# Attention with normalized q and k: shifted fp16 patterns as 64-bit adds on GpSimd, the rest of its work on VectorE

## The chip, the cores and the metric

The kernel runs on one core of a Trainium2 chip. The metric is the device time in microseconds, the median of the runs. A profiled execution is taken beside them; its rows give the engines' instructions with start and duration. The engines are TensorE (PE in the profile, PEld its weight loads), VectorE (DVE), ScalarE (ACT), GpSimd (POOL) and SyncE (SP), which here only issues DMAs.

## The reference

32 heads, 2048 positions, head dimension 20, bfloat16. Rows of q and k are normalized to length one, the scores are scaled by a factor per head, and plain attention follows:

```python
qn = q / (jnp.sqrt((q * q).sum(axis=-1, keepdims=True)) + eps)
kn = k / (jnp.sqrt((k * k).sum(axis=-1, keepdims=True)) + eps)
logits = jnp.einsum('bhqd,bhkd->bhqk', qn, kn) * t[None, :, None, None]
attn = _softmax(logits, axis=-1)
return jnp.einsum('bhqk,bhkd->bhqd', attn, v)
```

Scores are bounded by t, a little above 1, so the kernel takes no maximum. v has a column of ones beside it (`vaug`), so that the product with the exponentials yields the row sums too, and the division comes at the end.

## The kernel before

**Two ways to an exponential.** Each head's 2048 x 2048 scores are cut into 16 tiles by key block; a tile is 128 keys by 2048 queries, in four groups of 512 queries. TensorE makes the scores (L762). For most tiles ("A") ScalarE takes the exp out of PSUM into `p_ring` (L853), in waves of two and three groups in turn (128x1024 and 128x1536). For the others ("D") VectorE makes a cheap exponential: it reads the scores out of PSUM, two instructions of 128x1024 a tile, and writes an int16 which is, read as fp16, a piecewise linear power of two (`xt`, L909). To smooth it, three more patterns are made by adding 256, 512 and 768 to that integer (`ss`, L916, one instruction of 128x2048 each), that is the same curve shifted in phase; they are multiplied with copies of v scaled by 2^(-phase/1024) (`vph`, L577), and TensorE adds all four products up in `psO` (L782). `DVE_TILES` says how many of the 16 tiles of each head are D tiles: 158 in all, the other 354 are ScalarE's.

**GpSimd's part.** A shift may also go to GpSimd (`f.alt`, L920): two int16 lanes are added at once as one int32, as a tensor-tensor add whose second operand is a constant of `add_w` with step zero; so a tile of 2048 int16 is 1024 words, and it may be cut into pieces of at least 128 words. GpSimd also scales the copies of v (`vs`, L577, three a head), folds the squares of q and k twice before VectorE sums them (`fold`, L615), normalizes q and k from head 3 on (`norm`, L657) and divides by the row sums (`fin`, L806, heads 1 to 30).

**The order of work** is written out ahead of time by a list scheduler in the kernel's own file (`Program`): each task has an engine, a duration, dependences and a due time in units of heads (`pri`, small is early), and each engine then runs its tasks in the scheduler's order, with semaphore waits for the dependences. So every engine's queue is strictly in order: an instruction that waits holds all behind it. `pool_fill` places GpSimd's work: a piece is given to GpSimd when VectorE begins an instruction that reads PSUM (`t1`, L909), a transpose (`tr`, L795) or a sum (`su`, L622), and it is cut to the length which should end with that instruction (`piece`, 0.02 us and `PRATE` us a word, after 0.3 us of lead, or none where the wait can be taken earlier); VectorE's other instructions start, in the plan, only after such a piece. A shift goes to GpSimd only if VectorE has other work waiting (`KEEP`).

**Preparation of a head** runs some three heads ahead (`LEAD` 3.2): loads, squares (L607), sums, an inverse square root in integer and float steps (L626 to L644), normalization, then on SP's queue a transposing DMA into `qkT` (L675) and DMAs that lay out `qz` and the rotated copies `kR`. From head 5 on two heads are prepared together. v is loaded into one of six buffers; the scaled copies follow.

The lines that the change and the prediction's steps touch: L577 (`vs`), L615 (`fold`), L622 (sum), L657 and L664 (`norm` on GpSimd and on VectorE), L806 (`fin`), L916 and L920 (shift on VectorE and on GpSimd), L909 (PSUM read), L853 (exp).

Of the kernel before, what the change touches and what calls it, by code (L numbers as in the profile page):

```python
# [11 lines left out]
F32 = mybir.dt.float32  # L12
I32 = mybir.dt.int32
I16 = mybir.dt.int16
ACT = mybir.ActivationFunctionType
AXIS_X = mybir.AxisListType.X

# [2 lines left out]

KEXP = 0.2403756
PHASES = (256, 512, 768)
LOG2E = math.log2(math.e)
RS_MAGIC = 1594963007.0
RS_K1 = -2.253391575687845
# [20 lines left out]
class Program:  # L46
# [12 lines left out]
    PE_REST = 4.2  # L59
    PV_SLACK = 0.6  # L60
    OVER = 0.03
    PRATE = 0.00164
    KEEP = 0.3
    RESTP = 0.3
    SPARE = 0.0
# [10 lines left out]
    def add(self, eng, name, fn, dur, deps=(), pri=0.0, lat=0.0, dma=None):  # L76
        t = Task(eng, name, fn, dur, deps, pri, lat, dma)
        self.tasks.append(t)
        return t
# [310 lines left out]
def bass_standalone__qk_norm__prompt_kernel(  # L390
# [17 lines left out]
    NV = 6  # L408
# [14 lines left out]
    PE_MM = 0.23  # L423
    MORE = 12
    DLM = 2
    DVE_TILES = [4, 4, 4, 5, 4, 5, 5, 5, 5, 5, 5, 5, 5, 5, 6, 5, 5, 6, 5, 5, 3, 5, 5, 5, 6, 5, 4, 6, 5, 5, 6, 5]
    NDMAX = 6
    NPOOL, FPOOL = True, True
    FUSE, FOLD = True, 2
    NQ, NSQ, NSTEP = 2, 4, 0.0  # L430
    EXP0 = 0.051
    RSPOOL = False
    RTPOOL = False
    VPRI = 0.3
    LGATE = 0
    TTRATE = 0.00168
    TTDUR, TTWIN = 0.8, 0.55
# [2 lines left out]
    with ExitStack() as es:  # L440
        sbuf = lambda name, shape, dt: es.enter_context(nc.sbuf_tensor(name, shape, dt))
# [3 lines left out]
        t_f32 = sbuf("t_f32", [128, H], F32)  # L445
        act_scr = sbuf("act_scr", [128, 32], F32)
        ones = sbuf("ones", [128, 512], BF16)
        add_w = sbuf("add_w", [128, len(PHASES)], I32)
        ident = sbuf("ident", [128, 128], BF16)
        qk_sb = sbuf("qk_sb", [128, NB * 2 * R, D], BF16)  # L450
        vaug = [sbuf(f"vaug{i}", [128, R, 32], BF16) for i in range(NV)]
# [10 lines left out]
        xt = [sbuf("xt", [128, NX * 2048], I16)]  # L462
# [10 lines left out]
        add = prog.add  # L473
# [4 lines left out]
        def memset(eng, ap, val, dur, pri):  # L478
            return add(eng, "z", lambda e, tk: e.memset(ap, val), dur, pri=pri)
# [20 lines left out]
        while not waves or waves[-1][-1] < NA - 1:  # L500
            i = waves[-1][-1] + 1 if waves else 0
# [3 lines left out]
        for h in range(H):  # L505
            i = d0[h]
# [11 lines left out]
        add("ACT", "warm", lambda e, tk: e.activation(act_scr[:, :], act_scr[:, :], ACT.Exp), 1.5, [scr0], -95)  # L518
        ld_t = dma("SP", "ld_t", tb16[:, :], bass.AP(t.tensor, 0, [[0, 128], [1, H]]), [], -40, "t")
        z_one = memset("DVE", ones[:, :], 1.0, 0.2, -99)  # L520
        for i, x in enumerate(PHASES):
            memset("POOL", add_w[:, i:i + 1].bitcast(I16), x, 0.1, -98)
        z_id = add("POOL", "id", lambda e, tk: e.affine_select(
            ident[:, :], ones[:, 0:128], [[1, 128]], ALU.is_equal, 0.0, base=0, channel_multiplier=-1), 0.5, [z_one], -99)
        z_kx = memset("DVE", kx[:, :].rearrange("p (r w) -> p r w", w=32)[:, :, D:32], 0.0, 0.5, -97)
# [6 lines left out]
        z_v = []  # L532
# [6 lines left out]
        lds, ld_v, norm, trn, rot = {}, {}, {}, {}, {}  # L539
# [14 lines left out]
        def add_loads(h):  # L554
            b, bv = (h + 1) % NB, h % NV
            pri = h - LEAD - 0.5
            war = (norm[h - NB] if h >= NB else []) + ([lambda: [trn[max(h - 3, 0) if h < 5 + LGATE else h - 4]]] if h >= EARLY else [])
            x = qk_of(h)
            lds[h] = [dma("SP", f"ldk{h}", x[:, R:2 * R, :], k[0, h].rearrange("(p r) d -> p r d", p=128),
                          war, pri - 0.01 if h else -50, f"k{b}", lat=4.5 if h else 2.2, dur=0.5)]  # L560
            if h == 0:
                lds[h].append(dma("ACT", "ldq0", x[:, 0:R, :], q[0, 0].rearrange("(p r) d -> p r d", p=128),
                                  [], -99, "q0a"))
            else:

                for nh in range(4):
                    src = bass.AP(q.tensor, q[0, h].offset + nh * D,
                                  [[16 * D, 32], [4 * D, 4], [512 * D, 4], [1, D]])
                    dst = x[32 * nh:32 * nh + 32, 0:R, :].rearrange("p (c g) d -> p c g d", g=4)
                    lds[h].append(dma("SP", f"ldq{h}", dst, src, war, pri, f"q{b}", lat=4.5, dur=0.68))  # L570
            war = (pv_users[h - NV] if h >= NV else z_v[bv]) + ([lambda: [trn[h - 2]]] if h >= 2 else [])
            if h == 1:
                war = war + [lambda: [trn[0]]]
            ld_v[h] = dma("SP", f"ldv{h}", vaug[bv][:, :, 0:D], v[0, h].rearrange("(p r) d -> p r d", p=128),
                          war, pri + VPRI, f"v{bv}", lat=2.6, dur=1.4)
            nd = 4 if h < DLM else DVE_TILES[h]
            vsc[h] = [add("POOL", f"vs{h}", lambda e, tk, i=i: e.tensor_scalar(  # L577
                vph[bv][:, i, 0:nd, :], vaug[bv][:, R - nd:R, :], 2.0 ** (-PHASES[i] / 1024.0), 1.0, ALU.mult, ALU.mult),
                0.4, [ld_v[h]] + (pv_users[h - NV] if h >= NV else z_v[bv]), pri + 0.2) for i in range(len(PHASES))]
            for u in vsc[h] if h else []:  # L580
                u.win = 0.14

        def add_prep(hs):
            due = hs[0] - LEAD if hs[0] != 1 else FIRST
# [293 lines left out]
        def add_dgroup(jg):  # L878
            js = D_groups[jg]
            sx = se = 0  # L880
            ox, oe = place(0, NX, len(js)), place(1, NE, len(js))
            bx, be = 2048 * ox, 2048 * oe
            w = 2048 * len(js)
            old = lambda n, i: last_use.get((n, (ox if n == "x" else oe) + i), [])
            new = {}
            t1s = []
            for i, j in enumerate(js):
                h, rg = D_tiles[j]
                due = h + (j - d0[h] + 0.3) / DVE_TILES[h] - DLEAD
                n1 = W1 // 512  # L890
                for k in range(0, NG, n1):
                    gs = GORD[k:k + n1]
                    slot = nchunk[0] % (1024 // W1)
                    nchunk[0] += 1

                    def f_qk(eng, rows, h=h, rg=rg, gs=gs, slot=slot):
                        last = None
                        for m, g in enumerate(gs):
                            o = slot * W1 + 512 * m
                            last = qk_mm(eng, h, rg[g], g, psD[:, o:o + 512], rows)  # L900
                        return last
                    deps = [t1_prev.get(nchunk[0] - 1024 // W1)] + (q0 if j == 0 else [])
                    for g in gs:
                        deps += qk_deps([(h, rg[g], g)])
                    qk = add("PE", f"qkD{j}.{k}", lambda e, tk, f=f_qk: f(e, tk.rows), PE_MM, deps, due - 20000.0)
                    qk.modes = [("q2", 64, PE_MM, 256.0 * n1), ("qk", 128, PE_MM * n1, 512.0 * n1)]
                    qk_users[h].append(qk)
                    o = bx + 2048 * i + 512 * k
                    t1_prev[nchunk[0]] = add("DVE", f"t1.{j}.{k}", lambda e, tk, o=o, slot=slot: e.tensor_scalar(  # L909
                        xt[sx][:, o:o + W1], psD[:, slot * W1:slot * W1 + W1], X_MUL, X_ADD, ALU.mult, ALU.add),  # L910
                        0.067 + W1 / 960.0, [qk] + old("x", i), due - 5)
                    t1s.append(t1_prev[nchunk[0]])
            sh = []
            for i in range(len(PHASES)):
                dst, w = ss[i][0], 2048 * len(js)
                f = add("DVE", f"s{i}.{js[0]}", lambda e, tk, i=i, dst=dst: e.tensor_scalar(  # L916
                    dst[:, be:be + w], xt[0][:, bx:bx + w], float(PHASES[i]), None, ALU.add), 0.068 + w / 3840.0,
                    t1s + [u for m in range(len(js)) for u in old(f"s{i}", m)], due)
                if len(js) == 1 and jg >= 2:
                    f.alt = lambda c, n, i=i, dst=dst: lambda e, tk: e.tensor_tensor(  # L920
                        dst[:, be + 2 * c:be + 2 * (c + n)].bitcast(I32), xt[0][:, bx + 2 * c:bx + 2 * (c + n)].bitcast(I32),
                        bass.AP(add_w, i, [add_w[:, :].ap[0], [0, n]]), ALU.add)
                sh.append([(list(range(len(js))), f)])
            for m in range(len(js)):
                new["x", ox + m] = [u for us in sh for ms, u in us if m in ms]
            for i, j in enumerate(js):
                h, rg = D_tiles[j]
                for nm, tile, dep, ph in [("x", xt[sx], t1s[2 * i:2 * i + 2], None)] + [
                        (f"s{n}", ss[n][se], [u for ms, u in sh[n] if i in ms], n) for n in range(len(PHASES))]:
                    p = add("PE", f"pv{nm}{j}", lambda e, tk, h=h, rg=rg, o=2048 * i + (bx if ph is None else be), tile=tile, ph=ph: pv_mm(  # L930
                        e, h, lambda g: rg[g],
                        lambda g: tile[:, o + 512 * GORD[g]:o + 512 * GORD[g] + 512].bitcast(FP16), ph),
                        PE_MM, dep + pv_base(h) + (vsc[h] if ph is not None else []), due + 0.2)
                    pv_users[h].append(p)
                    new.setdefault((nm, (ox if nm == "x" else oe) + i), []).append(p)
            last_use.update(new)
# [76 lines left out]
```

## Time and profile before

| | us |
|---|---|
| median of 3 runs | 655.32 (655.14 to 655.39) |
| the profiled execution's span | 654.0 |
| first exp starts, last exp ends, in it | 8.42, 649.65 |
| GpSimd busy with shift pieces (L920, 314 pieces) | 311.4 |
| GpSimd busy with normalization (L657), folds (L615), v copies (L577), division (L806) | 47.7, 44.8, 40.0, 27.4 |
| VectorE busy with PSUM reads (L909), shifts (L916) | 384.8, 239.1 |

In the profile's groups a row gives line, engine, operation, the tiles written and read, the commonest shape and the count; then the time that the group was busy, the mean of one in ns, and the engine's idle time before them with what ended it. In the timeline a row gives start and duration in us. The TensorE clock row gives the granted clock in 40 slices, 9 for full speed.

### The profile page before, as it was taken

Reading aid. Unit: us, or ns where it says so; the run is one execution under the profiler, and the core shown is the slowest. Engines: PE = TensorE matmul, PEld = TensorE weight load, DVE = VectorE, ACT = ScalarE, POOL = GpSimd, SP = SyncE. Lnnn points to the kernel's source line nnn. Section 1 sums busy time; section 2 is a strip of 40 time slices with the busy share of each in tenths; the row PEclk is TensorE's granted clock in tenths of the full one; section 3 lists DMA queues with packets and bytes.
Section 4 is the critical chain, followed back from the end, with each engine's and each line's share of the span. In section 5 each row is a group of like instructions: output and inputs, shape, how many; then the busy total and the mean of one; then the engine's idle time right before and its main releaser. Section 6 shows DMA issues by size and latency. Waiting matters only on the chain.

```text
span 654.0 us, 14865 instructions
## 1 busy us (share of the span) xinstructions
PE 590.3 (90%) x5991; PEld 168.9 (26%) x6019; DVE 646.1 (99%) x911; ACT 647.4 (99%) x576; POOL 472.7 (72%) x550
## 2 busy tenths in 40 slices
PE   8888889899899898899999998989999989989997
PEld 2222222222222222222222222222222222222222
DVE  8999999999999999999999999999999999999998
ACT  9999999999999999999999999999999999999997
POOL 2577765777778776777877767768787876777773
PEclk9999999999999999999999989999999999999999
DMA  5554435342431535325242251354304334040200
GB/s 65 81 71 64 74 55 81 45 81 22 83 57 27 92 37 74 48 56 75 32 87 31 54 76 27 73 62 74 55 18 81 42 66 64 18 85 12 49 13 11
DMA packets 196724, 36.25 MB, mean 55 GB/s; under 512 B 172592, under 2 KB 196656, under 8 KB 196656
## 3 DMA queue, kind: packets, MB, share of 16 engines
q1 hardware_dynamic: 196512, 35.22, 35.0%
q8 instruction: 47, 0.77, 0.5%
q14 instruction: 21, 0.17, 0.1%
q10 hardware_dynamic: 144, 0.08, 0.0%
HBM read 7.87 MB, written 2.62 MB: 16 GB/s over the span
## 4 chain that ended last, share of the span: by engine, by line
ACT 97%; PE 2%; DVE 0%; issue 0%; ACTq 0%
ACT p_ring L853 96%; PE psO L782 1%; PE psA L762 1%; ACT qz L529 0%; ACT L518 0%; PE psD L762 0%; ACT qz L730 0%; DVE oT L795 0%; ACT xq L697 0%; DVE o_stage L806 0%; ACTq L476 0%; ACT qkT L725 0%; DVE rec L798 0%; ACT act_scr L518 0%; ACT t_f L536 0%
## 5 line engine op out<-in xcount | busy, mean ns | idle before, releaser
L853 ACT ACTIVATE p_ring<-psA 128x1024 bf16<-128x1024 f32 (+1 forms) x567 | 640.3, 1436 | 1.0 <-PE psA L762 0.9
L909 DVE TENSOR_SCALAR xt<-psD 128x1024 int16<-128x1024 f32 x316 | 384.8, 1218 | 2.8 <-PE psD L762 1.5
L920 POOL TENSOR_TENSOR ss<-xt,add_w 128x672 int32<-128x672 int32 (+16 forms) x314 | 311.4, 999 | 102.3 <-DVE ss L916 57.8
L762 PE MATMUL psA<-qz,kR 32*128 32x512 bf16 (+2 forms) x1045 | 215.5, 386 | 40.4 <-ACT p_ring L853 33.5
L916 DVE TENSOR_SCALAR ss<-xt 128x2048 int16<-128x2048 int16 x359 | 239.1, 681 | 0.0
L782 PE MATMUL psO<-ss,vph 128*32 128x512 f16 x1896 | 169.7, 385 | 0.0
L762 PE MATMUL psD<-qz,kR 64*128 64x512 bf16 (+1 forms) x469 | 121.7, 385 | 6.8 <-DVE xt L909 5.3
L782 PE MATMUL psO<-p_ring,vaug 128*32 128x512 bf16 x1416 | 127.8, 385 | 0.0
L762 PE MATMUL psA<-qz,qkT 32*128 32x512 bf16 (+2 forms) x349 | 114.3, 385 | 9.9 <-ACT p_ring L853 8.1
L762 PEld LDWEIGHTS psA<-qz,kR 32*128 32x128 bf16 (+2 forms) x1062 | 52.3, 92 | 174.5 <-ACT p_ring L853 173.6
L577 POOL TENSOR_SCALAR vph<-vaug 128x160 f16<-128x160 bf16 (+3 forms) x96 | 40.0, 417 | 33.8 <-DMA vaug<-in_v_dram 12.7
L782 PE MATMUL psO<-xt,vaug 128*32 128x512 f16 x632 | 62.3, 387 | 0.0
L782 PEld LDWEIGHTS psO<-ss,vph 128*32 128x32 f16 x1896 | 43.6, 94 | 69.5 <-issue 56.6
L762 PE MATMUL psD<-qz,qkT 64*128 64x512 bf16 (+1 forms) x157 | 59.3, 386 | 1.3 <-DVE xt L909 1.0
L657 POOL TENSOR_TENSOR qkn<-qk_sb,rs_r 128x640 bf16<-128x640 bf16 x29 | 47.7, 1644 | 11.4 <-DVE ss L916 5.1
L782 PEld LDWEIGHTS psO<-p_ring,vaug 128*32 128x32 bf16 x1416 | 34.2, 94 | 56.9 <-issue 48.1
L762 PEld LDWEIGHTS psD<-qz,kR 64*128 64x128 bf16 (+1 forms) x474 | 29.9, 93 | 73.5 <-DVE xt L909 55.5
L762 PEld LDWEIGHTS psA<-qz,qkT 32*128 32x128 bf16 (+2 forms) x354 | 27.6, 92 | 56.7 <-ACT p_ring L853 54.7
L615 POOL TENSOR_TENSOR fold<-sq 128x320 f32<-128x320 bf16 x29 | 27.5, 951 | 13.8 <-DVE ss L916 7.3
L806 POOL TENSOR_TENSOR o_stage<-oT,rec 128x320 bf16<-128x320 f32 x30 | 27.4, 913 | 9.4 <-DVE ss L916 7.1
L795 DVE STREAM_TRANSPOSE oT<-psO 128x512 f32<-128x512 f32 x32 | 22.6, 708 | 0.9 <-PE psO L782 0.9
L782 PEld LDWEIGHTS psO<-xt,vaug 128*32 128x32 bf16 x632 | 16.3, 94 | 27.6 <-issue 22.2
(49 smaller groups left out, 115.0 us busy)
## 6 DMA issues: line engine op xcount, KB each, us to landing
kR<-qkT SPq DMA_DIRECT2D x62, 96.0 KB, 2.1
qz<-qkT SPq DMA_DIRECT2D x124, 32.0 KB, 1.8
kR<-qkT SPq DMA_DIRECT2D x62, 64.0 KB, 2.0
qk_sb<-in_k_dram SPq DMA_DIRECT2D x32, 80.0 KB, 2.5
vaug<-in_v_dram SPq DMA_DIRECT2D x32, 80.0 KB, 3.5
qk_sb<-in_q_dram SPq DMA_DIRECT2D x124, 20.0 KB, 2.5
out_dram<-o_stage SPq DMA_DIRECT2D x31, 80.0 KB, 2.6
kR<-qkT SPq DMA_DIRECT2D x62, 32.0 KB, 1.9
```

What stands on the lines that cost most here:

```text
L577: vsc[h] = [add("POOL", f"vs{h}", lambda e, tk, i=i: e.tensor_scalar(vph[bv][:, i, 0:nd, :], vaug[bv][:, R - nd:R, :], 2.0 ** (-PHASES[i] ...
L615: c2.append(pool("fold", lambda e, tk, a=a, k=k, at=at: e.tensor_tensor(at[k + 1][0][:, a:a + 2 * R, :], at[k][0][:, a:a + 2 * R, 0:at[k + ...
L657: u = add("POOL", f"norm{h}", lambda e, tk, x=x, b=b, i=i, j=j: e.tensor_tensor(qkn[b][:, j:j + m, 0:D], x[:, j:j + m, :], bc(rs["r"][:, 2 ...
L762: return eng.matmul(dst, lhsT, mov, tile_position=(p0, 0))
L782: last = eng.matmul(psO[32 * g:32 * g + 32, :], w, rhs_of(g), start=start, stop=False, skip_group_check=True, tile_position=(0, 32 * g))
L795: trO[h] = add("DVE", f"tr{h}", lambda e, tk: e.transpose(oT[:, :, :].rearrange("p r d -> p (r d)"), psO[:, :]), 0.63, [lambda: pv_users[h ...
L806: fin[h] = add("POOL" if pool else "DVE", f"fin{h}", lambda e, tk: e.tensor_tensor(st, src, rb, ALU.mult), TTDUR if pool else 0.40, [rc] + ...
L853: act[w] = add("ACT", f"exp{w}", lambda e, tk: e.activation(p_ring[:, p0 * 512:p0 * 512 + n], psA[:, slot * WAVES[0] * 512:slot * WAVES[0] ...
L909: t1_prev[nchunk[0]] = add("DVE", f"t1.{j}.{k}", lambda e, tk, o=o, slot=slot: e.tensor_scalar(xt[sx][:, o:o + W1], psD[:, slot * W1:slot ...
L916: f = add("DVE", f"s{i}.{js[0]}", lambda e, tk, i=i, dst=dst: e.tensor_scalar(dst[:, be:be + w], xt[0][:, bx:bx + w], float(PHASES[i]), No ...
L920: f.alt = lambda c, n, i=i, dst=dst: lambda e, tk: e.tensor_tensor(dst[:, be + 2 * c:be + 2 * (c + n)].bitcast(I32), xt[0][:, bx + 2 * c:b ...
```

## The change

GpSimd's shift becomes a 64-bit integer add of a constant carried in the instruction: four int16 lanes at once, the same bytes (`c` and `n` still count 32-bit words, so that a whole tile is 512 elements of 64 bits). The constants in `add_w` and their memsets go. The scheduler's price of a word (`PRATE`) goes from 0.00164 to 0.00085 us. All of GpSimd's other steady work moves to VectorE: the normalization (`NPOOL`), the division (`FPOOL`), the scaled copies of v (due 1.5 instead of 0.2 heads after the load's own due time, `VSP`), and the two folds are left out, so that the sum reads the squares in full (`FOLD`). `DVE_TILES` has 159 instead of 158 tiles: one more in heads 12, 13 and 29, one less in heads 15 and 21.

```diff
--- before.py
+++ after.py
@@ -12,6 +12,7 @@
 F32 = mybir.dt.float32
 I32 = mybir.dt.int32
 I16 = mybir.dt.int16
+I64 = mybir.dt.int64
 ACT = mybir.ActivationFunctionType
 AXIS_X = mybir.AxisListType.X
 
@@ -20,6 +21,7 @@
 
 KEXP = 0.2403756
 PHASES = (256, 512, 768)
+LANES = 0x0001000100010001
 LOG2E = math.log2(math.e)
 RS_MAGIC = 1594963007.0
 RS_K1 = -2.253391575687845
@@ -59,7 +61,7 @@
     PE_REST = 4.2
     PV_SLACK = 0.6
     OVER = 0.03
-    PRATE = 0.00164
+    PRATE = 0.00085
     KEEP = 0.3
     RESTP = 0.3
     SPARE = 0.0
@@ -423,15 +425,16 @@
     PE_MM = 0.23
     MORE = 12
     DLM = 2
-    DVE_TILES = [4, 4, 4, 5, 4, 5, 5, 5, 5, 5, 5, 5, 5, 5, 6, 5, 5, 6, 5, 5, 3, 5, 5, 5, 6, 5, 4, 6, 5, 5, 6, 5]
+    DVE_TILES = [4, 4, 4, 5, 4, 5, 5, 5, 5, 5, 5, 5, 6, 6, 6, 4, 5, 6, 5, 5, 3, 4, 5, 5, 6, 5, 4, 6, 5, 6, 6, 5]
     NDMAX = 6
-    NPOOL, FPOOL = True, True
-    FUSE, FOLD = True, 2
+    NPOOL, FPOOL = False, False
+    FUSE, FOLD = True, 0
     NQ, NSQ, NSTEP = 2, 4, 0.0
     EXP0 = 0.051
     RSPOOL = False
     RTPOOL = False
     VPRI = 0.3
+    VSP = 1.5
     LGATE = 0
     TTRATE = 0.00168
     TTDUR, TTWIN = 0.8, 0.55
@@ -445,7 +448,6 @@
         t_f32 = sbuf("t_f32", [128, H], F32)
         act_scr = sbuf("act_scr", [128, 32], F32)
         ones = sbuf("ones", [128, 512], BF16)
-        add_w = sbuf("add_w", [128, len(PHASES)], I32)
         ident = sbuf("ident", [128, 128], BF16)
         qk_sb = sbuf("qk_sb", [128, NB * 2 * R, D], BF16)
         vaug = [sbuf(f"vaug{i}", [128, R, 32], BF16) for i in range(NV)]
@@ -518,8 +520,6 @@
         add("ACT", "warm", lambda e, tk: e.activation(act_scr[:, :], act_scr[:, :], ACT.Exp), 1.5, [scr0], -95)
         ld_t = dma("SP", "ld_t", tb16[:, :], bass.AP(t.tensor, 0, [[0, 128], [1, H]]), [], -40, "t")
         z_one = memset("DVE", ones[:, :], 1.0, 0.2, -99)
-        for i, x in enumerate(PHASES):
-            memset("POOL", add_w[:, i:i + 1].bitcast(I16), x, 0.1, -98)
         z_id = add("POOL", "id", lambda e, tk: e.affine_select(
             ident[:, :], ones[:, 0:128], [[1, 128]], ALU.is_equal, 0.0, base=0, channel_multiplier=-1), 0.5, [z_one], -99)
         z_kx = memset("DVE", kx[:, :].rearrange("p (r w) -> p r w", w=32)[:, :, D:32], 0.0, 0.5, -97)
@@ -574,11 +574,9 @@
             ld_v[h] = dma("SP", f"ldv{h}", vaug[bv][:, :, 0:D], v[0, h].rearrange("(p r) d -> p r d", p=128),
                           war, pri + VPRI, f"v{bv}", lat=2.6, dur=1.4)
             nd = 4 if h < DLM else DVE_TILES[h]
-            vsc[h] = [add("POOL", f"vs{h}", lambda e, tk, i=i: e.tensor_scalar(
+            vsc[h] = [add("DVE", f"vs{h}", lambda e, tk, i=i: e.tensor_scalar(
                 vph[bv][:, i, 0:nd, :], vaug[bv][:, R - nd:R, :], 2.0 ** (-PHASES[i] / 1024.0), 1.0, ALU.mult, ALU.mult),
-                0.4, [ld_v[h]] + (pv_users[h - NV] if h >= NV else z_v[bv]), pri + 0.2) for i in range(len(PHASES))]
-            for u in vsc[h] if h else []:
-                u.win = 0.14
+                0.11, [ld_v[h]] + (pv_users[h - NV] if h >= NV else z_v[bv]), pri + VSP) for i in range(len(PHASES))]
 
         def add_prep(hs):
             due = hs[0] - LEAD if hs[0] != 1 else FIRST
@@ -917,9 +915,9 @@
                     dst[:, be:be + w], xt[0][:, bx:bx + w], float(PHASES[i]), None, ALU.add), 0.068 + w / 3840.0,
                     t1s + [u for m in range(len(js)) for u in old(f"s{i}", m)], due)
                 if len(js) == 1 and jg >= 2:
-                    f.alt = lambda c, n, i=i, dst=dst: lambda e, tk: e.tensor_tensor(
-                        dst[:, be + 2 * c:be + 2 * (c + n)].bitcast(I32), xt[0][:, bx + 2 * c:bx + 2 * (c + n)].bitcast(I32),
-                        bass.AP(add_w, i, [add_w[:, :].ap[0], [0, n]]), ALU.add)
+                    f.alt = lambda c, n, i=i, dst=dst: lambda e, tk: e.int64_add(
+                        dst[:, be + 2 * c:be + 2 * (c + n)].bitcast(I64), xt[0][:, bx + 2 * c:bx + 2 * (c + n)].bitcast(I64),
+                        PHASES[i] * LANES)
                 sh.append([(list(range(len(js))), f)])
             for m in range(len(js)):
                 new["x", ox + m] = [u for us in sh for ms, u in us if m in ms]
```

## The prediction

> **What bounds the kernel now.** I read the chain of waits first, because it says which engine's work adds up to the end, and then the engine totals.
>
> ```profile
> PE 590.3 (90%) x5991; PEld 168.9 (26%) x6019; DVE 646.1 (99%) x911; ACT 647.4 (99%) x576; POOL 472.7 (72%) x550
> PEclk9999999999999999999999989999999999999999
> ...
> ACT 97%; PE 2%; DVE 0%; issue 0%; ACTq 0%
> ```
>
> ScalarE is the chain: its exps run from 8.42 us to 649.65 us of the 654.0 us span (timeline), so the span is 8.4 of start, 641.2 of exps, 4.4 of last transpose, divide and store. VectorE is at 99% too, so it is a second bound just below the first. The groups and the timeline give the prices:
>
> ```profile
> L853 ACT ACTIVATE p_ring<-psA 128x1024 bf16<-128x1024 f32 (+1 forms) x567 | 640.3, 1436 | 1.0 <-PE psA L762 0.9
> L909 DVE TENSOR_SCALAR xt<-psD 128x1024 int16<-128x1024 f32 x316 | 384.8, 1218 | 2.8 <-PE psD L762 1.5
> L920 POOL TENSOR_TENSOR ss<-xt,add_w 128x672 int32<-128x672 int32 (+16 forms) x314 | 311.4, 999 | 102.3 <-DVE ss L916 57.8
> L916 DVE TENSOR_SCALAR ss<-xt 128x2048 int16<-128x2048 int16 x359 | 239.1, 681 | 0.0
> ```
>
> ```profile
> 308.63 0.32 POOL L577 TENSOR_SCALAR vph<-vaug 128x160 f16<-128x160 bf16 x1
> 312.16 0.88 POOL L920 TENSOR_TENSOR ss<-xt,add_w 128x416 int32<-128x416 int32 x1
> ...
> 331.24 1.04 POOL L920 TENSOR_TENSOR ss<-xt,add_w 128x512 int32<-128x512 int32 x1 [0.78 <-DVE ss L916]
> ```
>
> ```profile
> 311.81 1.22 DVE L909 TENSOR_SCALAR xt<-psD 128x1024 int16<-128x1024 f32 x1
> ...
> 312.95 0.21 DVE L636 SCALAR_TENSOR_TENSOR rs_y<-rs_b 128x64 f32<-128x64 f32 x1
> 313.08 0.69 DVE L916 TENSOR_SCALAR ss<-xt 128x2048 int16<-128x2048 int16 x1
> ...
> 313.68 1.22 DVE L909 TENSOR_SCALAR xt<-psD 128x1024 int16<-128x1024 f32 x1
> ```
>
> VectorE's instructions overlap by some 0.08 us, so a duration is not a cost; start to start is. A PSUM read (L909) costs 312.95 - 311.81 = 1.14, a shift (L916) 313.68 - 313.08 = 0.60. I take 0.08 off every VectorE duration below. GpSimd's shift pieces end inside the PSUM reads and seldom inside a shift: the schedule puts them there, and I call a PSUM read a "shadow". There are 316 x 1.14 + 32 transposes x 0.63 = 380 us of it.
>
> **ScalarE: the gain.** The tile list sums to 159 instead of 158. One tile is four 128x512 units of the 1416 that ScalarE takes. (649.65 - 8.42) / 1416 = 0.453 us a unit, so ScalarE loses 1.8 us of work. Nothing else in the diff touches it.
>
> **VectorE: what is added.** Rows of its own for the moved work, minus 0.08:
>
> ```profile
> L664 DVE TENSOR_TENSOR qkn<-qk_sb,rs_r 128x640 bf16<-128x640 bf16 x2 | 1.6, 818 | 0.0
> L806 DVE TENSOR_TENSOR o_stage<-oT,rec 128x320 bf16<-128x320 f32 x2 | 1.0, 484 | 0.0
> L622 DVE TENSOR_REDUCE rs_sum<-fold 128x64 f32<-128x320 f32 x13 | 6.1, 472 | 0.0
> L622 DVE TENSOR_REDUCE rs_sum<-sq 128x32 f32<-128x640 bf16 x3 | 2.5, 817 | 0.1
> ```
>
> Normalization: 29 heads x 0.74 = 21.4 us. Division by the row sums: 30 x 0.40 = 12.0. Without the two folds the sum reads 1280 elements a pair instead of 320: (817 - 472) / 320 = 1.08 ns an element, so 960 x 1.08 = 1.03 more for 13 pairs, and 0.51 more for three single heads: 14.9. The scaled copies of v: 96 of 128x160. VectorE has no such row. The nearest, its 128x128 and 128x256 copies in bf16 (188 and 218 ns), give 0.11 to 0.14 each; at one element a cycle, the 1.08 above, it is 0.2 to 0.25. That is 11 to 24 us; I take 11, since the copies are the same kind of one-input, 16-bit, SBUF-to-SBUF work. The extra tile brings two PSUM reads, 2.3. Together 61.6 us, and VectorE must also end 1.8 earlier: 63.4 us of shifts have to leave it, 63.4 / 0.60 = 105 of its 359. There are 3 x 159 = 477 shift tiles, so GpSimd must make 223, where it now makes 474 - 359 = 115.
>
> **GpSimd: can it?** Now: (1.04 - 0.88) / 96 = 1.67 ns a 32-bit word and 0.19 us fixed, for an add with two inputs. A one-input operation with a constant shows in the 128x160 row (0.32) and in the 128x96 one (0.271, by form): 0.83 ns an element, 0.19 fixed. The 64-bit add with a constant has no row. Bounds: 0.42 ns a word if the 0.83 holds for an 8-byte element, 1.67 if nothing is gained. I take 0.83 a word: one input as in the v rows, and twice the bytes of a 32-bit element. A whole tile of 1024 words is then 0.19 + 0.85 = 1.04 us, which fits one shadow of 1.14. 223 tiles cost 232 us whole, some 275 cut in two. At present the shadows take 115 x 1024 x 1.67 = 197, 314 pieces x 0.19 = 60, normalization 29 x 1.25, division 30 x 0.72, folds 29 x 1.24 and v copies 96 x 0.32: 380 in all, as much as there is. So at 0.83 the plan fits with room, at 0.42 (136 us) with more, and at 1.67 (424) not.
>
> [...]
>
> **Edits at nothing.** The three pattern memsets at the start go: GpSimd waits for v there. The v copies now stand in VectorE's queue behind v's load. GpSimd waited 12.7 us for it in three times at the start, hidden since nobody else was behind. On VectorE everything would be behind: PSUM reads, then TensorE, then the exps. The schedule holds these copies back by 1.3 heads more than before (VSP against 0.2), some 27 us at 654 / 32 a head, so I take 0; bounds 0 and 12.7. SP issues the same DMAs; only the transposes' wait changes engine (140.8 us behind GpSimd's normalization now), three heads, 60 us, ahead of use.
>
> **Sum.** 654.0 - 1.8 = 652.2 for a profiled execution; the median of the runs shown lies 1.3 above it, so **653.5 us**. ScalarE's small stalls are assumed as before: undisturbed its two sizes step by 1.330 and 0.904, 283 x 2.234 = 632.2, so 8.1 us of the 640.3 are stalls, 1.4 of them where the clock fell to 0.5 at 378 us.
>
> **Rivals.**
> 1. The stalls shrink too. For: shadows are asked for 275 of 380 us instead of all, so patterns arrive earlier; one more tile loads TensorE a little. Against: most stalls come behind TensorE's own score matmuls for VectorE, which stay. Without the clock drop and with a quarter of the other 6.7: 653.5 - 1.4 - 1.7 = 650.4.
> 2. Slower: the handover between the two engines. VectorE has no idle time; every piece that ends late holds its next shift, then the PSUM reads, then TensorE's queue and the exps. For: a 64-bit piece is planned to fill a shadow almost wholly (1.04 in 1.14), and the end of a piece is seen up to 0.11 us after the shadow's. Against: today 359 shifts take only 5 us more than 359 x 0.60. Over 223 pieces it undoes the gain from 8 ns each and is slower by over 0.2% from 14; at 25 ns it costs 5.6: 659.1. If the v copies cost the upper 24 us, VectorE is 13 us behind unless GpSimd takes it, which gives the same side.
> 3. The 64-bit add saves nothing a word: 223 x 0.86 = 192 us of overrun, less what shadow is free (380 - 275 = 105): 87 and up, some 740.
> 4. VectorE waits for v at the start: up to 12.7, say 6: 659.5.
>
> **How the numbers follow.** Forecast 0.47, own range 652.0 to 655.2; rival 1 0.21; rival 2 0.24; rival 3 0.03; rival 4 0.05. The predicted time is the forecast's. The range takes rival 1 and most of 2 and 4: 650.0 to 659.0; what is left out is rival 3 and the ends. 0.2% is 1.3 us, about what a measurement of this kernel can tell: faster is below 654.0. The forecast's 0.47 is 0.36 faster, 0.11 same; rival 1 faster; of 2 and 4 0.04 are same; the rest is slower: 0.57, 0.15, 0.28.
>
> **What would show it.** ScalarE with about 1412 / 2.5 = 565 exps, idle under 2 us; 318 PSUM reads; shifts on VectorE near 254; GpSimd with 64-bit adds alone, whole tiles near 1.04 us when not held, busy 230 to 350 us. Wrong: shifts starting late behind GpSimd, their step above 0.62 on the mean (rival 2); pieces of 1.9 us (rival 3); VectorE idle before a v copy (rival 4); two or more clock drops; VectorE's count far from 254 with the v copies above 0.14.

## The result, and the profile after

| | before | after |
|---|---|---|
| median of the runs, us | 655.33 | 660.07 (659.43 to 661.13) |
| ratio to before, 95% interval | | 1.0073 [1.0059, 1.0087] |
| the profiled execution's span | 654.0 | 659.4 |
| first exp starts | 8.42 | 14.81 |
| 25th exp starts | 35.26 | 42.27 |
| last exp ends | 649.65 | 654.96 |

The changed kernel is slower by 0.73% where 0.28% faster was forecast. The profiled execution after is the slowest of its four (661.13 us), so its span differs by 5.4 us where the medians differ by 4.7. The table holds the whole story in three rows: from the 25th exp to the end of the last one, before takes 614.39 us and after 612.69. That is 1.70 less, against the 1.8 that the prediction took for the one tile fewer on ScalarE; each of the two profiles has one fall of TensorE's clock in that stretch, to 0.5 for 3.4 us (at 377.8 before, at 439.2 after). The first 42 us give back 7.0.

Engine totals, TensorE's clock and the chain of waits, from the page of the kernel after:

```profile
PE 598.5 (91%) x6031; PEld 167.6 (25%) x6031; DVE 644.7 (98%) x966; ACT 646.3 (98%) x574; POOL 303.7 (46%) x270
...
PEclk7999999999999999999999999989999999999999
...
ACT 93%; PE 3%; DVE 1%; DMA 1%; issue 1%; POOL 0%; DVEq 0%
```

ScalarE works 1.1 us less than before (646.3 against 647.4) in a span that is 5.4 longer: it is idle more, and its share of the chain falls from 97 to 93%. GpSimd has gone from 72 to 46%. The first slice of the clock row is 7 instead of 9. The groups of the steady work show nothing wrong:

```profile
L851 ACT ACTIVATE p_ring<-psA 128x1024 bf16<-128x1024 f32 (+1 forms) x565 | 639.0, 1438 | 4.9 <-PE psA L760 4.6
L918 POOL INT64_ADD ss<-xt x250 | 300.5, 1203 | 339.3 <-DVE xt L907 64.9
L907 DVE TENSOR_SCALAR xt<-psD 128x1024 int16<-128x1024 f32 x318 | 387.5, 1219 | 3.6 <-PE psD L760 2.4
...
L914 DVE TENSOR_SCALAR ss<-xt 128x2048 int16<-128x2048 int16 x257 | 174.0, 684 | 0.2
```

The exps' idle time behind TensorE has grown from 0.9 to 4.6. A few long waits are in question, then, rather than many small ones. In the list of waits of the kernel after (engine, line, what it waited for: us in total, times, longest) three stand out in which one wait is all or most of the total:

```profile
POOL ident L523 <- issue: 7.1, 1, 7.1
DVE vph L577 <- DMA vaug<-in_v_dram: 6.2, 1, 6.2
...
ACT p_ring L851 <- PE psA L760: 4.6, 2, 3.7
```

L523 is GpSimd's select that makes the identity matrix for TensorE's transposes; the change does not touch that line. GpSimd's timeline (start, duration, instruction, idle time before it) in the kernel before:

```profile
1.56 0.29 POOL L523 TENSOR_SCALAR_AFFINE_SELECT ident<-ones 128x128 bf16<-128x128 bf16 x1 [0.27 <-DVE ones L479]
1.80 0.77 POOL L479 MEMSET qkn<- 128x384 bf16 x2
2.51 1.63 POOL L479 MEMSET vaug<- 128x176 bf16 x12
```

and in the kernel after:

```profile
8.65 0.28 POOL L523 TENSOR_SCALAR_AFFINE_SELECT ident<-ones 128x128 bf16<-128x128 bf16 x1 [7.10 <-issue]
8.90 0.41 POOL L481 MEMSET qkn<- 128x384 bf16 x1
9.26 1.61 POOL L481 MEMSET vaug<- 128x176 bf16 x12
```

For 7.10 us GpSimd does nothing and waits for nothing that the profile names ("issue"). In the kernel after, the records of L523 show two of its sequencer's configuration instructions (MODIFY_POOL_CONFIG, 11 ns each) at the front of that gap, at 1.6 us; before, the same two stand at 1.2 and 1.3 and the select follows 0.3 later. Two others stand ahead of the 64-bit adds of L918, at 11.0. Everything behind the select is 7 us late: the identity, and the clearing of v's buffers. The chain of waits of the kernel after in its first 25 us (start, us, what) goes through both:

```profile
6.76 1.89 issue
8.65 0.28 POOL ident L523
8.93 0.37 POOL qkn L481
9.31 0.32 POOL vaug L481 x3
9.62 3.34 DMA vaug<-in_v_dram
...
12.98 0.40 DVE vph L577 x3
...
13.42 0.70 DVE qz L731
...
14.16 0.61 PE psA L760 x2
```

v's load may start only when its buffer is cleared (9.62), lands 3.34 later, VectorE makes the scaled copies, and only then the casts of q that the scores wait for. A second way leads through SP's queue, whose rows of v's first load and of the transposing DMAs into `kR` are, before:

```profile
3.64 0.64 SPq L476 DMA_DIRECT2D vaug<-in_v_dram  x1
...
9.56 3.93 SPq L743 DMA_TRANSPOSE kR<-kx  x3
```

and after:

```profile
9.62 0.62 SPq L478 DMA_DIRECT2D vaug<-in_v_dram  x1
...
16.19 3.93 SPq L741 DMA_TRANSPOSE kR<-kx  x3
```

On SP, too, everything behind v's load comes later: three loads of q, one of k, four more of q and then the transposes stand there. The load of k goes out at 12.86 instead of 6.22, and the transposes are 6.6 us later too.

### The profile page after: what moved, and what is told of

The parts are those of the page before. It is cut to its first block, busy times and chain, and to the rows that moved or that the text cites. A ratio compares the mean times of both kernels' runs of the same rounds, so it can differ in the third digit from the quotient of the medians.

```text
span 659.4 us, 14668 instructions
## 1 busy us (share of the span) xinstructions
PE 598.5 (91%) x6031; PEld 167.6 (25%) x6031; DVE 644.7 (98%) x966; ACT 646.3 (98%) x574; POOL 303.7 (46%) x270
## 4 chain that ended last, share of the span: by engine, by line
ACT 93%; PE 3%; DVE 1%; DMA 1%; issue 1%; POOL 0%; DVEq 0%
ACT p_ring L851 93%; PE psO L780 1%; PE psA L760 1%; DMA vaug<-in_v_dram 1%; PE psD L760 0%; DMA qk_sb<-in_k_dram 0%; DVE xt L907 0%; PE psO L722 0%; DVE sq L605 0%; DVE rs_sum L620 0%; DVE oT L793 0%; DVE qz L731 0%; DVE ss L914 0%; DVE vph L577 0%; DVE kx L699 0%
## 5 line engine op out<-in xcount | busy, mean ns | idle before, releaser
L918 POOL INT64_ADD ss<-xt x250 | 300.5, 1203 | 339.3 <-DVE xt L907 64.9
L760 PE MATMUL psA<-qz,kR 32*128 32x512 bf16 (+2 forms) x1059 | 219.5, 386 | 33.5 <-ACT p_ring L851 29.2
L914 DVE TENSOR_SCALAR ss<-xt 128x2048 int16<-128x2048 int16 x257 | 174.0, 684 | 0.2
L780 PE MATMUL psO<-ss,vph 128*32 128x512 f16 x1908 | 162.5, 384 | 0.0
L780 PEld LDWEIGHTS psO<-ss,vph 128*32 128x32 f16 x1908 | 41.2, 94 | 68.7 <-issue 57.9
L662 DVE TENSOR_TENSOR qkn<-qk_sb,rs_r 128x640 bf16<-128x640 bf16 x31 | 25.2, 814 | 0.0
L620 DVE TENSOR_REDUCE rs_sum<-sq 128x64 f32<-128x1280 bf16 (+1 forms) x19 | 24.0, 1266 | 0.1
L577 DVE TENSOR_SCALAR vph<-vaug 128x160 f16<-128x160 bf16 (+3 forms) x96 | 15.1, 193 | 6.2 <-DMA vaug<-in_v_dram 6.2
L760 PEld LDWEIGHTS psD<-qz,qkT 64*128 64x128 bf16 (+1 forms) x159 | 14.4, 93 | 18.1 <-DVE xt L907 13.9
```

The source lines that it names most:

```text
L577: vsc[h] = [add("DVE", f"vs{h}", lambda e, tk, i=i: e.tensor_scalar(vph[bv][:, i, 0:nd, :], vaug[bv][:, R - nd:R, :], 2.0 ** (-PHASES[i] / ...
L620: sums.append(dv("sum", lambda e, tk, i=i, m2=m2, src=src: e.tensor_reduce(rs["sum"][:, 2 * R * i:2 * R * i + m2], src, AXIS_X, ALU.add), ...
L662: norm[h] = [dv("norm", lambda e, tk, x=x, b=b, i=i: e.tensor_tensor(qkn[b][:, :, 0:D], x[:, :, :], bc(rs["r"][:, 2 * R * i:2 * R * (i + 1 ...
L760: return eng.matmul(dst, lhsT, mov, tile_position=(p0, 0))
L780: last = eng.matmul(psO[32 * g:32 * g + 32, :], w, rhs_of(g), start=start, stop=False, skip_group_check=True, tile_position=(0, 32 * g))
L918: f.alt = lambda c, n, i=i, dst=dst: lambda e, tk: e.int64_add(dst[:, be + 2 * c:be + 2 * (c + n)].bitcast(I64), xt[0][:, bx + 2 * c:bx + ...
```

## The experiments

The theory (A): GpSimd loses the 7 us where it has to go from the 64-bit add, on which an execution ends, back to the select near the start of the next, and what queues behind the select carries the delay to the exps. The expectations below name a load of code as the reason; that was assumed, no row of the traces shows one. The rival (B): VectorE's own wait for v, the prediction's rival 4, is what costs. A second rival (C): the steady work loses, by the handover between VectorE and GpSimd, the prediction's rival 2. All kernels of this section compute the whole output. Each ratio is to runs of the kernel before that were taken beside it: their median is 655.56 us for e1 to e4, 655.44 for e5 and e6, 654.98 for e7.

**e1: the copies of v moved out of VectorE's way.** The kernel after, with the three scaled copies of head 0 behind the last of the casts of q.

```diff
+        o = prog.order["DVE"]
+        o[:] = [tk for tk in o if tk not in vsc[0]]
+        i = o.index(q0[3])
+        o[i + 1:i + 1] = vsc[0]
...
```

> The change with one edit: the three scaled copies of v of head 0 stand behind the two casts of q in VectorE's queue, everything else in the order of the change. Theory A (two causes in series at the start: GpSimd loads code for some 7 us before it makes the identity matrix, and VectorE then waits for v ahead of work that the first exp needs): the identity stays at 8.65 us, the casts follow it at about 9.6 instead of 13.42, the first exp comes at about 11.0 instead of 14.81, time 660.1 - 3.8 = 656.3. Theory B (the wait for v alone, the late identity costs nothing): first exp at 8.4 as before the change, 653.7. Theory C (the loss is in the steady state, by the handover between VectorE and GpSimd): unchanged, 660.

Measured: 660.45 us, 1.0078 [1.0061, 1.0095]; first exp 11.39, 25th 42.31. The first exp came 3.4 us earlier and the 25th did not move (42.27 in the kernel after). So A in the form in which it was expected here, two delays that add up and 656.3 us, fails. The 660 is what C foretold too, but from the 25th exp to the end of the last one e1 takes 612.65 us, as the kernel after does (612.69) and less than before (614.39), so C falls. SP's waits in the first 60 us, before and in e1, and a row of TensorE's timeline in e1 say why the 25th exp stayed:

```profile
SPq L476 <- POOL vaug L479: 0.6, 1, 0.6
...
SPq L478 <- POOL vaug L481: 7.3, 1, 7.3
```

```profile
19.11 0.61 PE L760 MATMUL psA<-qz,kR 32*128 32x512 bf16 x3 [1.35 <-DMA kR<-kx]
```

SP still stands 7.3 us behind the clearing of v's buffer (0.6 before), the transposes into `kR` still go out at 16.36, and the scores that need `kR` wait for them. VectorE's wait lay in the shadow of that: B falls as the cause, though its size was right.

**e2 and e3: no select.** The identity is put together from a row of ones and zeros that GpSimd writes and SP copies into the four diagonal blocks by DMA; the select is gone, so that GpSimd runs the 64-bit add and memsets alone. e3 has e1's move as well.

```diff
-        z_id = add("POOL", "id", lambda e, tk: e.affine_select(
...
+        z_f = memset("POOL", iflat[:, :], 0.0, 0.0, -100)
+        z_f1 = add("POOL", "z", lambda e, tk: e.memset(bass.AP(iflat, 0, [iflat[:, :].ap[0], [33, 32]]), 1.0), 0.0, [z_f], -99.9)
+        z_i = memset("POOL", ident[:, :], 0.0, 0.0, -99.8)
+        z_id = [dma("SP", f"id{g}", ident[32 * g:32 * g + 32, 32 * g:32 * g + 32],
+                    iflat[32 * g:32 * g + 1, :].rearrange("p (r c) -> p r c", c=32),
...
```

> The change with one edit: the identity matrix is made without GpSimd's select (memsets and four small DMAs), so that the 64-bit add is the only operation of GpSimd beside memsets; the copies of v stay ahead of the casts of q. Theory A: the gap of 7 us on GpSimd is gone, v's load is issued at 4 to 5 us and lands at 7.5 to 9, the casts of q follow the v copies at 8 to 9.5, the first exp comes at 9.2 to 10.7: 660.1 - 5.6 to - 4.1 = 654.5 to 656. Theory B: VectorE still waits for v as long as it did: 659 to 660. Theory C: 660.

> Both edits, the identity without GpSimd's select and the copies of v of head 0 behind the casts of q. Theory A: first exp at 8.4 to 8.8 us as before the change, and the rest as in the change: 653.7 to 654.1, that is 1.2 to 1.6 below the kernel before, which is the one tile less on ScalarE. Theory C: 659 or more.

Measured: e2 656.58, 1.0022 [1.0013, 1.0032], 25th exp 38.54; e3 657.96, 1.0035 [1.0022, 1.0048], 25th exp 38.39. GpSimd's gap is gone and with it, by the ratios of after and e2, 0.0051 x 655 = 3.3 us, but not the whole loss; both runs end above what was expected, e3 by some 4 us. The four DMAs now stand at the head of SP's queue. SP's timeline in e2:

```profile
2.38 2.52 SPq L479 DMA_DIRECT2D ident<-iflat  x4
...
6.29 0.64 SPq L479 DMA_DIRECT2D vaug<-in_v_dram  x1
...
13.48 3.94 SPq L746 DMA_TRANSPOSE kR<-kx  x3
```

The transposes are 3.9 us later than before, the 25th exp 3.3. In e3 the first exp is at 8.98, almost as before, but TensorE then waits 2.15 us for `kR` (at 16.04), and the 25th exp is hardly earlier than in e2: not the first score matters but the arrival of `kR`.

**e4: the kernel before, with one 64-bit add.** A test of A alone: the kernel before gets a single add of two words as GpSimd's last instruction. Nothing of the changed plan is in it.

```diff
...
+        add("POOL", "i64", lambda e, tk: e.int64_add(
+            scr64[:, 0:2].bitcast(I64), scr64[:, 0:2].bitcast(I64), 1), 0.3, [z_scr, fin[30]])
```

> The kernel before with one 64-bit add of two words on a scratch tile as GpSimd's last instruction of all, after the last division; nothing else is changed. Theory A in its stronger form (GpSimd holds the code of only one of the two kinds of operation, an execution that ends with the add finds the other kind gone when the next begins): the identity matrix is late by some 7 us though no add has run yet in this execution, the first exp comes at about 10.9 instead of 8.42 since no copy of v stands in VectorE's queue, time 655.3 + 2.5 = 657.8. Rival (the 7 us come of something else in the change, such as its other order of memsets): 655.3, or up to 0.5 more if the last add outlasts the last store.

Measured: 661.17 us, 1.0093 [1.0078, 1.0108]. GpSimd's timeline in e4, at its start and at its end:

```profile
8.57 0.28 POOL L525 TENSOR_SCALAR_AFFINE_SELECT ident<-ones 128x128 bf16<-128x128 bf16 x1 [7.29 <-issue]
...
658.16 0.18 POOL L960 INT64_ADD scr<-scr  x1 [6.04 <-issue]
```

One more instruction at the end of the kernel puts a gap of 7.29 us at its start, some 650 us ahead of that instruction. That an execution which ends on the add delays the first select of the next one would explain it. A gap ahead of the first operation in every kernel with both kinds, whichever ran last, would look the same here and was not tried apart. The add itself had to wait too, 6.04 us after the last division, which costs nothing there: the last exp ends 4.37 before the end of the span, as elsewhere (4.38 before). I had expected 657.8 from the late identity alone. The larger loss is that of the kernel after, by the same path: v's buffers are cleared late, SP stands 7.0 us behind them, TensorE waits 2.81 us for `kR`, and the 25th exp starts at 41.58.

**e6: the select stays, v's buffer is cleared ahead of it.** Only GpSimd's order changes (and the copies of head 0 go behind the last rotated copy), so the gap ahead of the select remains and SP no longer waits for it.

```diff
+        o = prog.order["POOL"]
+        m = z_v[0]
+        o[:] = m + [tk for tk in o if tk not in m]
...
+        i = max(i for i, tk in enumerate(o) if tk.name == "rotk0")
+        o[i + 1:i + 1] = vsc[0]
...
```

> The change with the select kept, and only the order of the start altered: GpSimd clears v's first buffer before it makes the identity matrix, so that SP's queue isn't held, and the copies of v of head 0 stand behind VectorE's work for the first rotated keys. Theory A2: the identity still comes at 8.7 to 9 us, the first exp at about 11.4, SP waits no more for GpSimd, the 25th exp at 37.8 to 38.8, time 655.5 - 1.7 + 2.5 to 3.5 = 656.3 to 657.3. If the place of v's load in SP's queue doesn't matter: 660, as with the copies of v moved alone.

Measured: 656.5 us, 1.0015 [1.0005, 1.0025]; first exp 11.34, 25th 38.48. GpSimd's timeline of e6:

```profile
0.78 0.35 POOL L481 MEMSET vaug<- 128x176 bf16 x2 [0.29 <-POOLq L1007]
...
8.77 0.28 POOL L523 TENSOR_SCALAR_AFFINE_SELECT ident<-ones 128x128 bf16<-128x128 bf16 x1 [6.96 <-issue]
```

The gap is as long as in the kernel after, and the time is less by 0.0058 of it. That part, 0.0058 x 655 = 3.8 us, was v's buffer in SP's queue: SP's wait for it is gone, the 25th exp moved by the same 3.8 (42.27 to 38.48), and moving the copies, by itself, had brought nothing in e1.

**e5 and e7: the identity on VectorE.** An index along the row, its transpose, and a comparison of the two in each diagonal block make the identity without the select and without a DMA. v's buffer is cleared early, as in e6, and some of VectorE's clearing goes to GpSimd. In e5 VectorE makes the index row by five doublings, in e7 GpSimd by 32 memsets:

```diff
-        z_id = add("POOL", "id", lambda e, tk: e.affine_select(
...
+        z_x = [memset("POOL", idx[:, i:i + 1], float(i), 0.0, -98.9) for i in range(32)]
+        z_t = add("DVE", "ix", lambda e, tk: e.transpose(idt[:, :], idx[:, :]), 0.0, z_x, -98.7)
+        z_i = memset("POOL", ident[:, :], 0.0, 0.0, -99)
+        z_id = [add("DVE", "id", lambda e, tk, g=g: e.tensor_tensor(
+            ident[32 * g:32 * g + 32, 32 * g:32 * g + 32], idx[32 * g:32 * g + 32, :], idt[32 * g:32 * g + 32, :], ALU.is_equal),
+            0.0, [z_t, z_i], -98.6) for g in range(4)]
...
```

> The change with its start mended on three engines and the order of all later work kept: the identity matrix comes from VectorE (a row of indices by doubling, a 32x32 transpose, four compares), so GpSimd has no select; three memsets of VectorE go to GpSimd to make room, with v's first buffer ahead of the rest; the copies of v of head 0 stand behind VectorE's work for the first rotated keys. No DMA is added, unlike in the two earlier versions without the select. Theory A2 (the start loses 7 us by one cause: the code load holds GpSimd's memsets, SP's queue waits with v's load for them, and the loads and the transposes of the first keys behind it come late; VectorE's own wait lies in the shadow of that): the first exp at 8.4 to 9, the 25th exp at 35.3 to 36 as in the kernel before (35.3) instead of 42.3, and 1.7 less from there to the last: 653.4 to 654.5 against 655.5 of the kernel before on this chip. Rival (the steady state loses by itself, through clock drops or the handover): the start as said, but 656 or more.

Measured: 655.86, 1.0005 [0.9996, 1.0014]; first exp 10.35, 25th 37.29. VectorE's timeline of e5 shows what was left:

```profile
1.48 2.79 DVE L527 TENSOR_SCALAR idx<-idx 128x1 f32<-128x1 f32 x5
4.30 0.21 DVE L529 STREAM_TRANSPOSE idt<-idx 128x32 f32<-128x32 f32 x1
4.55 0.83 DVE L531 TENSOR_TENSOR ident<-idx,idt 32x32 bf16<-32x32 f32 x4
5.41 0.49 DVE L614 TENSOR_TENSOR sq<-qk_sb 128x640 bf16<-128x640 bf16 x1
```

The five doublings took 2.79 us and pushed the first squares from 3.29 in the kernel after to 5.41; the first exp is late by about as much (10.35 against 8.42 before). The 655.86 misses the 653.4 to 654.5 that was expected. It is not that five small instructions are dear: the first took 0.15 us, the others 0.92, 0.35, 0.35 and 0.89, and each of these four ends 0.02 to 0.03 us after the end of a memset that GpSimd ran at the time. GpSimd's timeline of e5 in that stretch:

```profile
1.46 0.75 POOL L481 MEMSET kx<- 128x768 bf16 x1
...
2.14 1.18 POOL L481 MEMSET qkn<- 128x384 bf16 x3
...
3.27 0.98 POOL L481 MEMSET qz<- 128x1024 f32 x1
```

The three memsets of `qkn` end at 2.57, 2.94 and 3.32, that of `qz` at 4.24; the doublings end at 2.59, 2.97, 3.35 and 4.27. By these times it was the clearing moved to GpSimd to make room that held VectorE up.

> As the version with the identity from VectorE, but the row of indices is written by 32 small memsets on GpSimd instead of the chain of doublings on VectorE, which took 2.8 us and held the first squares (5.41 instead of 3.3 us). All later work keeps its order. Theory A2: the squares start at 3.3 again, the first exp at 8.4 to 8.6, the 25th at 35.3 to 35.7, and the stretch from there to the last exp lasts 611.6 without a clock drop as in the two runs before: 655.1 - 1.9 = 653.2 without a drop, 654.2 with one, against 655.4 of the kernel before: the tile's 1.7 is had. Rival: another wait takes its place at the start, as the chain of doublings did: 655 or more.

Measured: **653.34 us, 0.9978 [0.9969, 0.9987]** against 654.98 of the kernel before on the same chip; first exp 8.50, 25th 35.46. By the interval it is faster than the kernel before, by about 0.2%, and so than the kernel after. GpSimd's timeline of e7 has no gap at the start, and v's buffer is cleared at 2:

```profile
0.72 0.98 POOL L481 MEMSET idx<- 128x1 f32 x32 [0.29 <-POOLq L1013]
1.63 0.21 POOL L481 MEMSET ident<- 128x128 bf16 x1
1.77 0.35 POOL L481 MEMSET vaug<- 128x176 bf16 x2
```

and its groups show exps that wait for next to nothing:

```profile
L857 ACT ACTIVATE p_ring<-psA 128x1024 bf16<-128x1024 f32 (+1 forms) x565 | 638.4, 1436 | 0.1
```

With both ways out of the start closed, what is left comes near the prediction: a ratio of 0.9978 where 0.9972 was forecast. The loss of the kernel after, then, is the start's: by ratios, 0.0058 for v's buffer (after to e6) and 0.0037, 2.4 us, for the late identity (e6 to e7, which also moves some clearing to GpSimd); together 0.0095 of 655, 6.2 us. These shares include what TensorE's lower clock cost in the disturbed starts. e7's profiled span of 651.5 compares with 653.0 of the kernel before in runs in which its clock did not fall (654.0 in the one profiled): 1.5 less.

## Why the prediction was wrong

**What failed** is the part "Edits at nothing". It said "The three pattern memsets at the start go: GpSimd waits for v there", took the start as unchanged, and gave the v copies in VectorE's queue 0 with bounds of 0 and 12.7. Measured, the start costs 7.0 us by the 25th exp (35.26 to 42.27), by a gap of 7.10 us on GpSimd that no term of the sum stands for. Three things were missed in it. First, a new kind of instruction on GpSimd was priced by its duration alone; whether it would delay what GpSimd does at the start was not asked. The trace of before had the hint, two configuration records ahead of the select, but only in 0.3 us and with nothing to show that they could cost 7. Second, the reading that GpSimd's wait of 12.7 us for v was "hidden since nobody else was behind" looked at GpSimd's wait for the load and not at the load's wait for GpSimd: the load stands in SP's queue behind the clearing, and `kR` behind the load. Third, "The schedule holds these copies back by 1.3 heads more than before" is true of the due time, but head 0 has nothing to be held behind: its copies ran at 12.98, ahead of the casts of q. By itself this third miss cost nothing that the time shows (e1).

**Rival 4** (VectorE waits for v at the start, 659.5, chance 0.05) gave nearly the measured 660.07 and the sign that was named for it appeared, 6.2 us of idle time before a v copy. e1 shows that it is not the cause: without that wait the time is 660.45. That its number comes near is luck. A sign that appears as foretold can stand beside the cause rather than be it.

**What held.** ScalarE loses one tile: 565 exps, and 1.70 us less from the 25th exp on (1.8 predicted); in e7 2.81 less, of which some 1.1 (612.69 - 611.59) is a fall of the clock that the profiles of before and after have there and that of e7 has not. The 64-bit add takes 0.83 to 0.84 ns a 32-bit word (0.83 predicted): 1.04 us for a whole tile not held up (the first, at 29.99; 1.04 predicted) and 0.29 for the shortest piece, so rival 3 falls. On VectorE there are 257 shifts (254), 318 PSUM reads (318); start to start a normalization takes 0.73 (0.74), a division 0.40, a sum of a pair 1.39 (1.42), a v copy 0.110 (0.11 taken from the nearest row, 0.25 the other bound). GpSimd is busy 303.7 us (230 to 350); a typical piece takes 1.40 rather than 1.04, which cost nothing that the time shows and is taken up below. The step of VectorE's shifts, where the next instruction does not wait, is 0.602 at the median and 0.611 on the mean (0.612 before; 0.62 was the sign), so rival 2 falls; the exps' stalls shrink in no kernel by more than the clock's fall, so rival 1 does too.

What GpSimd's pieces lose beside VectorE's moved work comes to little. In the kernel after, the 34 that overlap a normalization or a squaring take 1.53 us at the median, 0.49 above a whole tile's 1.04, some 17 us of GpSimd's time, of which it had plenty.

The range failed for the same reason as its centre: the bound of 12.7 was there, but at a chance of 0.05, because the start had been looked at for what the diff's lines do and not for what stands behind them.

## What to carry to other kernels

When an engine gets a new kind of instruction, read what the profile shows ahead of it on that engine (two configuration records here), and look at the start of the execution as well as at the place where the instruction stands; in e4 a single instruction at the very end cost 5.6 us, and cost them at the start. Follow a delay at the start through every in-order queue, clearing, load, what is queued behind the load, and judge a repair by a late exp (the 25th here) rather than by the first, since the first can be saved and the next ones still wait. Where a steady gain is 1.8 us, the start has to be costed with the same care as the loop.

## What the runs showed of the hardware

**Two kinds of operation on GpSimd came with a gap at the start.** The gap ahead of the select is 7.10 us (after), 7.09 (e1), 7.29 (e4) and 6.96 (e6) where the kernel ends on a 64-bit add, and 0.27 in the kernel before, which has none; the add behind other work in e4 waited 6.04. Memsets stand ahead of the select without such a gap (0.29 us of idle time ahead of the first of the program's own, in before, after, e4 and e6), and in e7, where memsets and 64-bit adds are all that GpSimd does, they run from 0.72 on. So in the profiled executions the gap stands at the start where both kinds are used, and not where one kind is (before, e7). What fills it is in no row of the traces, and which of GpSimd's other operations would bring one beside the add was not tried apart.

**Instructions of GpSimd and VectorE took longer where they overlapped.** In the kernel after, the 69 of the 250 pieces that overlap no shift, normalization, squaring or division on VectorE take at most 1.04 us. The 141 that overlap a shift, the typical ones above, take 1.40 at the median, and the 34 that overlap a normalization or a squaring 1.53. In e5 VectorE's took longer, beside GpSimd's memsets: four doublings of 2 to 16 elements took 0.35 to 0.92 us, while the first, of one element, took 0.15 beside a memset that ran on for another 0.58.

**The clock was lower at a disturbed start.** In the kernel after, TensorE's granted clock was 0.5 from 9.1 to 19.4 us, and the score matmuls of 14.16 took 0.61 us instead of 0.39. It was 0.5 somewhere in the first 23 us of after and e1 to e4 and e6, and not in before, e5 and e7. What brings it about was not tried; its part of the loss stays within the sums above.
